# A fused attention and gated feed-forward kernel: output layer of tiles 2 to 8 in seven block products, mask as a matmul, new scheduler priorities

## Chip, cores and metric

The kernel runs on one core of one Trainium2 chip. The metric is the device time of one execution in microseconds. A profiled execution gives a span, from the first to the last instruction that the profile shows, and a time of its own that includes what lies around the span.

## What is computed

Causal attention with a sliding window of 64 over 8 batches of 8 heads, 576 positions and head size 64; then its output, as 4608 tokens by 512, goes through a gated feed-forward layer of width 1536. Inputs and output are float32. From the reference:

```python
scores = scale * np.matmul(q, k.transpose(0, 1, 3, 2))
rel = pos[:, None] - pos[None, :]
mask = (rel >= 0) & (rel < window)
scores = np.where(mask, scores, -1000000000.0)
...
attn = attn / (np.sum(attn, axis=-1, keepdims=True) + 1e-09)
...
x = np.ascontiguousarray(attn_out.transpose(0, 2, 1, 3)).reshape(B * S, H * D)
gate = np.maximum(x @ w_gate, 0.0)
val = x @ w_val
return (gate * val @ w_out).astype(np.float32)
```

## The kernel before

The 4608 tokens are nine tiles (0 to 8) of 512 tokens. For each tile there are three stages. *Attention* works on windows of 64 queries that see 128 keys: score matmuls for 8 windows of one half of the heads (`score_run`, L301) go to four PSUM banks, one for each of four heads, because a head's 64 channels lie as 32 rows times two and each row group of 32 rows is a head; ScalarE takes the exponential (L547), VectorE multiplies by the band of ones (L550), TensorE multiplies with the values (`value_block`, L310), VectorE divides by the row sums (L320) and transposes into the tile's activations `xt` (L325). *The hidden layer* (`fast_hidden`, L704) splits tokens, channels and hidden units in halves and makes both products, gate and value, by Winograd's form of Strassen's method: seven block products for eight, with differences of x (L619) and of the weights (L691) as operands. Its sums pass from PSUM through float32 buffers `pr`: ScalarE copies (L750), VectorE adds (L757), ScalarE applies the ReLU (L766, L788) and GpSimd multiplies gate and value into `g_sb` (L775). *The output layer* (`output`, L799) is a plain product: per 128 tokens 12 matmuls of 512 columns into one bank (L815), one copy by ScalarE (L824), one store issued by SyncE (L828). Tile 0 has its own way through the hidden layer (`direct_block`, L638), in which it waits for the weights to load, and the first 384 of its tokens are attended in `first_part` (L327), written out by hand; there the mask is added already in front of the scores, as a matmul of `ident` with `bias` (0 inside the band, -30000 outside).

All else is laid out by a planner (`Plan`, L39) while the program is built. Every operation has a key, a due time in microseconds; an engine that comes free in the planner's own clock takes the ready operation with the lowest key, if the PSUM banks and buffers that it takes are free. So keys are priorities: they set the order of the instructions on each engine, which on the chip is fixed. Keys are derived from `T1` and `STEP` (L127): tile t's hidden layer is due from `T1 + STEP (t - 1)`, its output is spread over the following step (L844). The planner also counts a port that VectorE and GpSimd share (L178). Eight PSUM banks are shared by everything, one of them first of all for the output; 12 buffers `p` hold weights of the attention, 12 float32 buffers `pr` the hidden layer's partial results, 3 float32 buffers `o_sb` the outputs.

GpSimd also issues the loads; SyncE issues the stores and the moves of values inside SBUF (L523).

## Time and profile before

| | us |
|---|---|
| median of 3 runs (313.9 to 316.3) | 314.2 |
| the profiled execution | 314.14 |
| its span | 312.4 |
| TensorE matmuls busy | 297.9 |
| GpSimd busy | 235.6 |
| VectorE busy | 231.8 |
| ScalarE busy | 212.1 |

Costliest groups, busy microseconds: GpSimd's products of gate and value (L775) 121.4 in 96; output matmuls (L815) 107.1 in 456; VectorE's sums (L757) 94.1 in 144; ScalarE's copies (L750) 80.0 in 144; the hidden layer's matmuls (L742) 201 in 1344, in four groups. The page calls TensorE's matmuls PE and its weight loads PEld, VectorE DVE, ScalarE ACT, GpSimd POOL, SyncE SP. A group's mean is how long one instruction lasts; matmuls overlap, so what one adds to a stream is less than its mean and is read from the length of a row of them.

### The profile page before, as it was taken

How to read it: one execution, taken by the hardware profiler on the slowest of the kernel's cores; microseconds unless marked ns; L12 is line 12 of the kernel's file. 1: busy time of each engine (PE TensorE's matmuls, PEld its weight loads, DVE VectorE, ACT ScalarE, POOL GpSimd, SP SyncE). 2: the span in 40 equal slices, each digit the busy share in tenths (PEclk: the TensorE clock that was granted, in tenths of full speed). 3: DMA queues.
4: the chain of work that ended last, by engine and by line, in shares of the span. 5: the costliest groups of instructions: out<-in, count | busy, mean ns of one | idle time of the engine just before them, and what ended most of it. 6: DMA issues, size and time to landing. Idle time of an engine off the chain costs nothing.

```text
span 312.4 us, 10351 instructions
## 1 busy us (share of the span) xinstructions
PE 297.9 (95%) x4341; PEld 213.6 (68%) x4341; DVE 231.8 (74%) x420; ACT 212.1 (68%) x414; POOL 235.6 (75%) x239
## 2 busy tenths in 40 slices
PE   4889989889999999999999999999999999999995
PEld 2566845767767776777777776776687777677754
DVE  6979999989979984799489948894687578524420
ACT  3544282878678669866887688658966986676641
POOL 8798995969997997699679966994569546945440
PEclk9999999999999999999999999999999999999999
DMA  7999999798259925984496549563010110000013
GB/s 218 187 196 208 186 207 209 165 140 69 50 97 196 114 67 106 171 114 66 86 186 94 75 75 162 83 80 70 36 38 36 37 36 36 36 34 36 34 67 103
DMA packets 56126, 32.81 MB, mean 105 GB/s; under 512 B 39440, under 2 KB 47504, under 8 KB 56080
## 3 DMA queue, kind: packets, MB, share of 16 engines
q0 software_dynamic: 46672, 18.29, 49.7%
q1 hardware_dynamic: 9408, 13.87, 13.7%
q8 instruction: 34, 0.56, 0.7%
q14 instruction: 12, 0.10, 0.1%
HBM read 37.75 MB, written 9.44 MB: 151 GB/s over the span
## 4 chain that ended last, share of the span: by engine, by line
PE 76%; DVE 11%; POOL 4%; DMA 3%; issue 3%; ACT 2%; ACTq 0%; POOLq 0%; DVEq 0%
PE bank L742 42%; PE bank L815 25%; PE bank L651 3%; DVE p L550 3%; PE bank L313 3%; DMA wv<-in_moe_w_val_dram 3%; PE bank L307 3%; DVE g_sb L662 2%; POOL v L286 2%; DVE qT L283 1%; POOL g_sb L775 1%; DVE kT L283 1%; DVE pr L757 1%; DVE xw L320 1%; DVE us L691 1%
## 5 line engine op out<-in xcount | busy, mean ns | idle before, releaser
L775 POOL TENSOR_TENSOR g_sb<-pr,pr 128x512 f16<-128x512 f32 x96 | 121.4, 1282 | 56.3 <-ACT pr L766 40.0
L757 DVE TENSOR_TENSOR pr<-bank,pr 128x512 f32<-128x512 f32 x144 | 94.1, 678 | 36.7 <-PE bank L742 31.3
L815 PE MATMUL bank<-wo,g_sb 128*128 128x512 f16 (+2 forms) x456 | 107.1, 368 | 0.2 <-POOL g_sb L775 0.2
L750 ACT COPY pr<-bank 128x512 f32<-128x512 f32 x144 | 80.0, 594 | 31.2 <-PE bank L742 24.6
L815 PEld LDWEIGHTS <-g_sb 128*128 128x128 f16 x456 | 43.3, 98 | 32.9 <-POOL g_sb L775 0.7
L742 PE MATMUL bank<-xt,us 128*128 128x256 f16 x384 | 57.2, 273 | 1.1 <-DVE pr L757 0.8
L742 PE MATMUL bank<-xt,vs 128*128 128x256 f16 x384 | 57.2, 273 | 0.0
L766 ACT ACTIVATE pr<-pr 128x512 f32<-128x512 f32 x72 | 45.9, 637 | 7.3 <-DVE pr L757 6.5
L550 DVE TENSOR_TENSOR p<-p,mask 128x512 f16<-128x512 f16 (+1 forms) x68 | 33.5, 518 | 22.7 <-ACT p L547 22.4
L742 PEld LDWEIGHTS <-us 128*128 128x128 f16 x384 | 36.7, 98 | 11.9 <-issue 1.0
L742 PE MATMUL bank<-xt,wg 128*128 128x256 f16 x288 | 43.3, 273 | 0.0
L742 PE MATMUL bank<-xt,wv 128*128 128x256 f16 x288 | 43.2, 273 | 0.0
L742 PEld LDWEIGHTS <-vs 128*128 128x128 f16 x384 | 37.0, 98 | 8.4
L824 ACT COPY o_sb<-bank 128x512 f32<-128x512 f32 (+2 forms) x38 | 21.6, 567 | 25.7 <-PE bank L815 24.7
L547 ACT ACTIVATE p<-bank 128x512 f16<-128x512 f32 (+1 forms) x68 | 36.0, 594 | 4.3 <-PE bank L307 4.0
L286 POOL DMA_DIRECT2D v<-in_v_dram x40 | 35.0, 878 | 0.2 <-issue 0.2
L788 ACT ACTIVATE pr<-bank 128x512 f32<-128x512 f32 x48 | 27.9, 600 | 9.2 <-PE bank L742 7.4
L742 PEld LDWEIGHTS <-wv 128*128 128x128 f16 x288 | 27.9, 98 | 5.3
L742 PEld LDWEIGHTS <-wg 128*128 128x128 f16 x288 | 27.1, 98 | 5.6 <-ACT pr L750 0.2
L320 DVE TENSOR_TENSOR xw<-bank,r 128x448 f16<-128x448 f32 (+2 forms) x45 | 25.7, 572 | 1.1
L325 DVE STREAM_TRANSPOSE xt<-xw 128x512 f16<-128x512 f16 (+2 forms) x38 | 25.6, 677 | 1.0 <-ACT xw L416 0.3
L619 POOL TENSOR_TENSOR xt<-xt 128x512 f16<-128x512 f16 x16 | 18.5, 1156 | 3.5 <-DVE r L566 3.5
(69 smaller groups left out, 253.4 us busy)
## 6 DMA issues: line engine op xcount, KB each, us to landing
out_dram<-o_sb SPq DMA_DIRECT2D x35, 256.0 KB, 2.3
k<-in_k_dram POOLq DMA_DIRECT2D x15, 288.0 KB, 6.2
q<-in_q_dram POOLq DMA_DIRECT2D x15, 288.0 KB, 6.9
v<-in_v_dram POOLq DMA_DIRECT2D x32, 128.0 KB, 4.9
v<-v SPq DMA_DIRECT2D x12, 132.0 KB, 2.5
v<-v SPq DMA_DIRECT2D x24, 66.0 KB, 2.0
wg<-in_moe_w_gate_dram POOLq DMA_DIRECT2D x6, 256.0 KB, 6.4
wv<-in_moe_w_val_dram POOLq DMA_DIRECT2D x6, 256.0 KB, 8.5
```

Source lines behind the costliest of these rows:

```text
L286: nc.gpsimd.dma_start(v16s[b % 2][lo:hi, g, :, 0:64], v[b, :, 64 * g - 64 + lo:64 * g - 64 + hi].rearrange("h p d -> p h d"))
L320: nc.vector.tensor_tensor(x, blocks_of(to, n)[:, :, 0:D].rearrange("p s (c e) -> p s e c", e=2), r[:, :, :, None].to_broadcast([128, n, 2, ...
L325: nc.vector.transpose(xt[:, 2 * hh:2 * hh + 2, c0:c0 + n].rearrange("p e (s c) -> p s e c", c=32), x)
L547: nc.scalar.activation(pp[g][:, 0:n].rearrange("p n c -> p (n c)"), st[g][:, 0:64 * n], ACT.Exp, scale=scale)
L550: VEC[e].tensor_tensor(pp[g][:, 0:n], pp[g][:, 0:n], mask[:, None, :].to_broadcast([128, n, 64]), MUL)
L742: nc.tensor.matmul(slot[to][:, HT * m:HT * m + HT], w[:, kk, 128 * m:128 * m + 128], x[:, kk], start=(first and m == 0 and kk == 0), stop= ...
L750: lambda e, hold=hold, slot=slot: nc.scalar.copy(hold["x"], slot["A"]),
L757: nc.vector.tensor_tensor(hold["x"], slot[to], hold["x"], ADD)
L766: lambda e: nc.scalar.activation(hold["x"], hold["x"], ACT.Relu), after=[o])
L775: lambda e: VEC[e].tensor_tensor(gh[:, fs:fs + 2, h], pair(a["x"]), pair(b["x"]), MUL),
L788: lambda e, hold=hold, slot=slot, i=i: nc.scalar.activation(hold["x"], slot["A"], ACT.Copy if i else ACT.Relu),
L815: nc.tensor.matmul(bank["b"][:, 0:c1 - c0], gs[t % 2][:, f, 128 * sub:128 * sub + 128], wo[:, f, c0:c1], start=(j == 0 and i == 0), stop=( ...
```

## The change

The output of tiles 2 to 8 is made by the same seven-product form (`fast_output`). With G the gated activations, split in halves of tokens and of hidden units (a11, a12 for the first 256 tokens, a21, a22 for the others), and W the output weights, split in halves of hidden units and of output channels (b11 to b22), it forms s1 = a21 + a22, s2 = s1 - a11, s3 = a11 - a21 (in the place of a21), s4 = a12 - s2 on VectorE, and once for all tiles four such sums of W (`w_sums`; one of them takes the place of b12). Each of the seven products is two groups of six matmuls of 256 columns. P1 = a11 b11, P6 = s2 t2, P7 = s3 t3 and P4 = a22 t4 gather in one bank (A), P2 = a12 b21 in a second, P5 = s1 t1 and P3 = s4 b22 in a third. ScalarE copies bank A after P1 and P6 and the third after P5, VectorE adds the other part from PSUM, and each quarter of the tile's output (256 by 256) is stored by itself; the last quarter of tile 8 in two pieces. The copies are held in the `pr` buffers, which tiles 0 and 1 now use for their outputs too; `o_sb` is gone, and `p` has 10 buffers for 12.

The mask of all other scores is now added as in `first_part`: eight matmuls per run put the transposed bias in front of the scores, so the multiplication on VectorE goes. The transposed bias is made once at the start. Values of one tile are chained in order. Nearly all keys are read from a table `K`; lines that differ in this alone are left out below, as are the names that follow from the rest.

```diff
@@ -16,6 +16,9 @@
+K = {"T1": 51.41, "STEP": 29.49, "wo1": 25.6, "wo2": 25.6, "q0": 3.01, "q1": 6.54, "q10": 3.96, "q11": 8.54, "v": 8.09, "v1": 9.34, "ql": 13.25, "qt": 9.67, "qti": 4.47, "vl": 12.65, "vc": 8.45, "vm": -3.3, "e": 2.08, "gap": 0.57, "gap1": -0.86, "r": -0.33, "tn": -0.21, "xf": 14.83, "wf": 1.51, "wfj": 2.98, "sn": 0.92, "su": 0.25, "re": 17.48, "mu": -1.5, "la": -9.73, "o0": 21.5, "o0j": 2.66, "o0s": -0.82, "oo": 0.049, "os": 0.292, "oj": 1.05, "gs": 0.96, "fo": 0.07, "fi": 0.074, "fs": 0.87, "fu": -1.36, "W0": 86.73, "TF": 2, "rs": 3.83, "rv": 12.34, "rt": -0.03, "d2": 10.31}
@@ -229,15 +232,16 @@
     kTs = [sb(f"kT{i}", [2, 64 + S, 2]) for i in range(2)]
     v16s = [sb(f"v16_{i}", [NG, H, VW]) for i in range(2)]
     nat = {(name, hh): sb(f"{name}{hh}", [S // 32 * D]) for name in "kq" for hh in range(2)}
-    ps = [sb(f"p{i}", [8, 64]) for i in range(12)]
+    ps = [sb(f"p{i}", [8, 64]) for i in range(10)]
     xw = sb("xw", [32, 2, D // 2])
     rw = [sb(f"r{i}", [32, 1], FP32) for i in range(2)]
     xs = [sb(f"xt{i}", [4, TT]) for i in range(4)]
     gs = [sb(f"g_sb{i}", [NF, TT]) for i in range(2)]
     prs = [sb(f"pr{i}", [TT], FP32) for i in range(12)]
-    os_ = [sb(f"o_sb{i}", [DM], FP32) for i in range(3)]
+    ss, ts = sb("ss", [3, HF, HT]), sb("ts", [3, HF, DM // 2])
     mask = consts.tile([128, 64], FP16)
     bias = consts.tile([128, 64], FP16)
+    biasT = consts.tile([128, 2, 128], FP16)
     ident = consts.tile([128, 128], FP16)
     zero = consts.tile([128, 512], FP16)
     zero32 = consts.tile([128, 384], FP32)
@@ -299,13 +303,21 @@
         return kTs[b % 2][rows, hh, 64 * w:64 * w + 128], qTs[b % 2][rows, hh, 64 * w:64 * w + 64]
 
     def score_run(st, items, biased=False):
+        n = len(items)
+        if not biased:
+            for s in range(2):
+                for g in range(G):
+                    rows = slice(32 * g, 32 * g + 32)
+                    nc.tensor.matmul(st[g][:, 0:64 * n].rearrange("p (n c) -> p n c", c=64)[:, :, 32 * s:32 * s + 32],
+                                     biasT[rows, s], ident[rows, None, rows].to_broadcast([32, n, 32]),
+                                     start=(s == 0), stop=False, skip_group_check=True)
         for i, (win, hh) in enumerate(items):
             for dh in range(2):
                 for g in range(G):
                     kk, qq = scores_of(win, hh, g)
                     c = 64 * i
                     nc.tensor.matmul(st[g][:, c:c + 64], kk[:, :, dh], qq[:, :, dh],
-                                     start=(dh == 0 and not biased), stop=(dh == 1), skip_group_check=biased)
+                                     start=False, stop=(dh == 1), skip_group_check=True)
 
     def value_block(to, c, p, win, hh, at, s):
         b, w = divmod(win, NG)
@@ -354,6 +366,12 @@
 
         st = banks[0:4], banks[4:8]
         rounded("k", nc.vector.tensor_copy, nc.scalar.copy)
+        for s in range(2):
+            for g in range(G):
+                nc.tensor.matmul(banks[6 + s][32 * g:32 * g + 32, 0:128], bias[:, 32 * s:32 * s + 32], ident,
+                                 start=True, stop=True, skip_group_check=True)
+        for s in range(2):
+            nc.scalar.copy(biasT[:, s], banks[6 + s][:, 0:128])
         for u in range(2):
             for g in range(G):
                 nc.tensor.matmul(st[u][g][:, 0:2 * U].rearrange("p (n c) -> p n c", c=64), ident,
...
@@ -450,8 +468,8 @@
             return pe(k * w * (n + 6) / 2400.0)
 
         T0 = 16.0
-        T1 = 49.0
-        STEP = 31.0
+        T1 = K["T1"]
+        STEP = K["STEP"]
 
         def period(t):
             return T1 + STEP * (t - 1)
...
@@ -537,20 +555,16 @@
             batches = sorted({w // NG for w, _ in items})
             halves = sorted({hh for _, hh in items})
             after = [turns[b, nm, hh] for b in batches if b for hh in halves for nm in "kq"]
-            run = op("scores", key, pe(0.0081 * 8 * n), lambda e: score_run([st[g] for g in range(G)], items),
+            run = op("scores", key, pe(0.0081 * 8 * n + 0.0268 * n), lambda e: score_run([st[g] for g in range(G)], items),
                      after=after, take=[("bank", st, range(G))])
             for b in batches:
                 score_ops[b].append(run)
-            masks = []
+            exps = []
             for g in range(G):
                 def exp(e, g=g):
                     nc.scalar.activation(pp[g][:, 0:n].rearrange("p n c -> p (n c)"), st[g][:, 0:64 * n], ACT.Exp, scale=scale)
-
-                def band(e, g=g):
-                    VEC[e].tensor_tensor(pp[g][:, 0:n], pp[g][:, 0:n], mask[:, None, :].to_broadcast([128, n, 64]), MUL)
-                x = op("exp", key + 0.8 + 0.6 * g, act(64 * n), exp, after=[run], take=[("p", pp, (g,))], give=[("bank", st, g)])
-                masks.append(op("mask", key + 2.0 + 0.8 * g, dve16(64 * n), band, after=[x]))
-            return pp, masks
+                exps.append(op("exp", key + K["e"] + 0.6 * g, act(64 * n), exp, after=[run], take=[("p", pp, (g,))], give=[("bank", st, g)]))
+            return pp, exps
 
         def value_bank(t, key, parts, before, gives, last):
 
...
@@ -822,14 +840,109 @@
 
                     def evac(e, bank=bank, o_sb=o_sb, c0=c0, c1=c1):
                         nc.scalar.copy(o_sb["o"][:, c0:c1], bank["b"][:, 0:c1 - c0])
-                    x = op("evac", key, act(c1 - c0), evac, after=before, take=[("o", o_sb, ("o",))], give=[("bank", bank, "b")])
+                    x = op("evac", key, act(c1 - c0), evac, after=before, take=[("pr", o_sb, ("o",))], give=[("bank", bank, "b")])
                     rows = slice(TT * t + 128 * sub, TT * t + 128 * sub + 128)
                     op("store", key + 0.5, {"SP": (0.35, False)},
                        lambda e, o_sb=o_sb, rows=rows, c0=c0, c1=c1: nc.sync.dma_start(out[rows, c0:c1], o_sb["o"][:, c0:c1]),
-                       after=[x], give=[("o", o_sb, "o")], dma=(0.26 * (c1 - c0) / DM, 0.3, "sp"))
-
-        last_part = []
-        output(0, lambda sub, j: T0 + 19.0 + 3.6 * j + 0.9 * sub, range(4))
+                       after=[x], give=[("pr", o_sb, "o")], dma=(0.26 * (c1 - c0) / DM, 0.3, "sp"))
+
+
+        low, high = slice(0, HF), slice(HF, NF)
+        HD = DM // 2
+        wsums = []
+
+        def w_sums():
+
+            b11, b12, b21, b22 = (wo[:, f, HD * d:HD * d + HD] for f in (low, high) for d in range(2))
+            before = [o for blk in range(NF // 4) for o in loaded["o", blk]]
+            direct_out = [o for t in range(TF) for o in out_ops[t]]
+            for c in range(NJ):
+                fs = slice(2 * c, 2 * c + 2)
+                made = []
+                for n, (to, x, y) in enumerate(((ts[:, 0], b12, b11), (ts[:, 1], b22, ts[:, 0]), (b12, b22, b12), (ts[:, 2], b21, ts[:, 1]))):
+                    after = before + [[], made[0:1], made[0:1] + direct_out, made[1:2]][n]
+                    made.append(op("wo_form", W0 + 4 * c + n, {**pool(512), **dve16(512)},
+                                   lambda e, to=to, x=x, y=y, fs=fs: VEC[e].tensor_tensor(to[:, fs], x[:, fs], y[:, fs], SUB), after=after))
+                wsums.extend(made)
+
+        def fast_output(t, key_of):
+
+            mine = out_ops.setdefault(t, [])
+            gt = gs[t % 2]
+            a11, a21, a12, a22 = (gt[:, f, HT * h:HT * h + HT] for f in (low, high) for h in range(2))
+            g11, g21, g12, g22 = ([gates[t, j, n, h] for j in range(NJ)] for n in range(2) for h in range(2))
+            done = out_ops.get(t - 1, [])
+            key = key_of(0)
+            sums = [[], [], [], []]
+            for c0, c1 in ([(2 * j, 2 * j + 2) for j in range(NJ)] if t == LAST else [(0, HF)]):
+                c = slice(c0, c1)
+                made = []
+                for n, (to, x, y, how) in enumerate(((ss[:, 0], a21, a22, ADD), (ss[:, 1], ss[:, 0], a11, SUB), (a21, a11, a21, SUB), (ss[:, 2], a12, ss[:, 1], SUB))):
+                    js = slice(c0 // 2, c1 // 2)
+                    after = [g21[js] + g22[js], g11[js] + made[0:1], g11[js] + made[0:1], g12[js] + made[1:2]][n] + done
+                    made.append(op("g_sum", key - K["gs"] + n, {"DVE": (0.11 + 0.0006 * (c1 - c0) * HT, True)},
+                                   lambda e, to=to, x=x, y=y, how=how, c=c: VEC[e].tensor_tensor(to[:, c], x[:, c], y[:, c], how), after=after))
+                    sums[n].append(made[n])
+            b11, b12, b21, b22 = (wo[:, f, HD * d:HD * d + HD] for f in (low, high) for d in range(2))
+            s1, s2, s3, s4 = sums
+            what = {"P1": (a11, b11, g11), "P2": (a12, b21, g12), "P3": (ss[:, 2], b22, s4), "P4": (a22, ts[:, 2], g22 + wsums),
+                    "P5": (ss[:, 0], ts[:, 0], s1 + wsums), "P6": (ss[:, 1], ts[:, 1], s2 + wsums), "P7": (a21, b12, s3 + wsums)}
+            bank, hold, snaps, ran = {}, {}, {}, {}
+            mine += [o for some in sums for o in some]
+
+            def leave(after, x, h, d, m0, m1, key):
+                rows = out[TT * t + HT * h + 128 * m0:TT * t + HT * h + 128 * m1, HD * d:HD * d + HD].rearrange("(m p) c -> p m c", p=128)
+                src = x["x"] if False else None
+                return op("store", key, {"SP": (0.35, False)},
+                          lambda e: nc.sync.dma_start(rows, x["x"][:, HD * m0:HD * m1].rearrange("p (m c) -> p m c", c=HD)),
+                          after=after, give=[("pr", x, "x")] if m1 == 2 else (), dma=(0.13 * (m1 - m0), 0.3, "sp"))
+
+            place = 0
+            for name in ("P1", "P2", "P6", "P5", "P7", "P3", "P4"):
+                a, b, after = what[name]
+                to = {"P2": "B", "P5": "C", "P3": "C"}.get(name, "A")
+                first = name in ("P1", "P2", "P5")
+                after = list(after)
+                if name in ("P6", "P7", "P3"):
+                    after.append(snaps[{"P6": "P1", "P7": "P6", "P3": "P5"}[name]])
+                if name == "P4":
+                    after += ran["C22"]
+                parts = []
+                for m in range(2):
+                    def mm(e, a=a, b=b, to=to, first=first, m=m):
+                        for f in range(HF):
+                            nc.tensor.matmul(bank[to][:, HD * m:HD * m + HD], a[:, f, 128 * m:128 * m + 128], b[:, f],
+                                             start=(first and m == 0 and f == 0), stop=(f == HF - 1), skip_group_check=True)
+                    k = key_of(place)
+                    place += 1
+                    parts.append(op("o" + name, k, direct(HD, 1, HF), mm, after=after + parts,
+                                    take=[("bo+bank" if to == "A" else "bank", bank, (to,))] if first and m == 0 else ()))
+                mine += parts
+                if name in ("P1", "P6", "P5"):
+                    x = hold[name] = {}
+                    snaps[name] = op("snap", k - K["fs"], act(512), lambda e, x=x, to=to: nc.scalar.copy(x["x"], bank[to]),
+                                     after=parts, take=[("pr", x, ("x",))])
+                    continue
+                src, h, d = {"P2": ("P1", 0, 0), "P7": ("P5", 1, 1), "P3": ("P6", 0, 1), "P4": (None, 1, 0)}[name]
+                x = hold.get(src, {})
+                ran[name] = []
+                for m0, m1 in ((0, 1), (1, 2)) if t == LAST and name == "P4" else ((0, 2),):
+                    c = slice(HD * m0, HD * m1)
+                    give = [("bank", bank, to)] if name != "P7" and m1 == 2 else ()
+                    if src:
+                        o = op("osum", k - K["fu"], dve(HD * (m1 - m0)),
+                               lambda e, x=x, to=to, c=c: nc.vector.tensor_tensor(x["x"][:, c], bank[to][:, c], x["x"][:, c], ADD),
+                               after=[snaps[src]] + parts[m0:m1], give=give)
+                    else:
+                        o = op("evac", k + 0.9, act(HD * (m1 - m0)), lambda e, x=x, to=to, c=c: nc.scalar.copy(x["x"][:, c], bank[to][:, c]),
+                               after=parts[m0:m1], take=[("pr", x, ("x",))] if m0 == 0 else (), give=give)
+                    if name == "P7":
+                        ran["C22"] = [o]
+                    leave([o], x, h, d, m0, m1, k + 0.5)
+
+        TF = int(K["TF"])
+        W0 = K["W0"]
+        output(0, lambda sub, j: T0 + K["o0"] + K["o0j"] * j + K["o0s"] * sub, range(4))
         made = 1
         for t in range(1, NT):
             while made < B and made * NG < 8 * t + 8:
@@ -841,10 +954,14 @@
             pieces = ((0, DM),)
             P = period(t + 1)
             if t < LAST:
-                output(t, lambda sub, j: P + STEP * (0.06 + 0.25 * sub) + 0.9 * j, range(4))
+                if t == TF:
+                    w_sums()
+                if t < TF:
+                    output(t, lambda sub, j: P + STEP * (K["oo"] + K["os"] * sub) + K["oj"] * j, range(4))
+                else:
+                    fast_output(t, lambda i: P + STEP * (K["fo"] + K["fi"] * i))
             else:
-                output(t, lambda sub, j: P + 2.7 * sub + 0.9 * j, range(3))
-                output(t, lambda sub, j: P + 2.7 * 3, range(3, 4), ((0, 256), (256, 384), (384, 512)))
+                fast_output(t, lambda i: P + 0.66 * i)
         end = plan.run(lambda o, e: o.fn(e))
         return plan
```

## Prediction

> **What bounds the kernel now.** I read the engines' totals, then busy time by stage, then the chain of work that ended last, then groups of instructions, and last the timeline for single intervals. The totals:
>
> ```profile
> PE 297.9 (95%) x4341; PEld 213.6 (68%) x4341; DVE 231.8 (74%) x420; ACT 212.1 (68%) x414; POOL 235.6 (75%) x239
> ```
>
> TensorE is busy 95% of the span; its weight loads lie beside its matmuls. Busy time by stage (length, then PE, PEld, DVE, ACT, POOL, each with its instructions):
>
> ```profile
> 0.00:18.50 18.50, 11.67 (x262) 6.92 (x263) 13.23 (x32) 8.71 (x28) 15.02 (x29) 1.00 1.28 199
> 18.50:40.00 21.50, 21.50 (x306) 16.31 (x303) 20.73 (x40) 8.99 (x20) 19.83 (x25) 1.00 1.39 199
> 40.00:59.00 19.00, 17.36 (x285) 10.45 (x283) 18.63 (x32) 10.94 (x20) 14.85 (x17) 1.00 1.20 202
> 59.00:90.46 31.46, 28.96 (x519) 21.65 (x518) 27.94 (x50) 24.86 (x49) 27.94 (x28) 1.00 0.65 84
> 90.46:122.18 31.72, 31.45 (x466) 22.42 (x464) 26.20 (x46) 23.15 (x46) 28.46 (x29) 1.00 0.75 119
> 122.18:153.90 31.72, 31.72 (x475) 23.22 (x473) 24.79 (x45) 23.75 (x46) 26.79 (x27) 1.00 0.76 111
> 298.69:312.40 13.71, 10.42 (x72) 5.91 (x70) 0.89 (x2) 3.30 (x7) 2.92 (x3) 1.00 0.26 90
> ```
>
> From 122 us to 298.7 PE never idles: a tile takes 31.72 us because that is its matmul work. PE idles 6.8 us in the first 18.5, then 1.64 + 2.50 + 0.27 = 4.4 us up to 122, and 3.3 us at the end. Between 18.5 and 90 us DVE is almost as full as PE; later it has 7 us free per tile. Is a busy PE at its pace? Pieces of the chain of waits (start, length, count):
>
> ```profile
> 134.49 4.37 PE bank L742 x40
> 298.69 7.79 PE bank L815 x36
> ```
>
> A 256-column matmul takes 4.37/40 = 0.1093 us, a 512-column one 7.79/36 = 0.2164. Time per column is the same, so columns are what costs. The clock column is 1.00 throughout.
>
> **The change, part by part**, against the profiled execution: span 312.40, 314.14 with the 1.74 around it (the median of the runs is 314.2).
>
> *Seven products for eight, tiles 2 to 8.* Per tile 48 matmuls of 512 columns, 48 x 0.2164 = 10.39 us, become 7 products x 2 token blocks x 6 = 84 of 256 columns, 84 x 0.1093 = 9.18. Their shape (128*128, 128x256 f16) is that of L742, so the price is a row of this trace. Tile 8, whose last block was cut in three, went from 10.42 to 9.18. 7 x 1.21 = **-8.5 us**, all on the path.
>
> *Mask in front of the scores.* Each run of scores (two per tile, 16 in all, and a half-size one for tile 0) gets 8 matmuls of 256 columns that contract 32 rows, in four row groups into four banks, like the scores behind them. The trace has no 256-column one of this kind. The nearest row is the score run itself:
>
> ```profile
> 157.32 0.68 PE L307 MATMUL bank<-qT,kT 32*128 32x64 f16 x64
> 157.93 0.61 PE L742 MATMUL bank<-xt,vs 128*128 128x256 f16 x4
> ```
>
> 64 matmuls of 64 columns, and the next begins 0.61 us after the first; less some 0.12 for leaving, 0.49. One at a time they would take 64 x 0.1093/4 = 1.75. Lower bound, four abreast: 2 x 0.109 = 0.22 per run; upper, one at a time: 0.87. I take 0.23, the scores' way: 16 x 0.23 + 0.12 = **+3.8 us** (3.6 to 14).
>
> The mask multiplications leave DVE (L550, 32.1 + 1.4 us). After 122 us that buys PE nothing directly. Values now wait for the exps alone.
>
> *New vector work per tile:* four f16 sums over 1536 elements on DVE and three additions out of PSUM (0.678 each by L757, 2.0 together). ACT has three copies and one eviction at 0.59 where it had four evictions. A clean 512-element f16 operation takes 0.42 us and a 256-element one 0.28 (shortest L550 records), so 1536 take 0.42 + 4 x 0.14 = 0.96, four 3.8. DVE goes from 24.8 to 24.8 - 3.5 (masks in one period) + 3.8 + 2.0 = 27.1 of a period of 31.72 - 1.21 + 0.46 = 31.0: covered by 3.9 us of slack. What eats that cover:
>
> ```profile
> L550 DVE TENSOR_TENSOR p<-p,mask 128x512 f16<-128x512 f16 x64 | 32.1, 528 | 22.2 <-ACT p L547 21.9
> 153.75 0.42 DVE L550 TENSOR_TENSOR p<-p,mask 128x512 f16<-128x512 f16 x1
> 44.69 2.40 DVE L550 TENSOR_TENSOR p<-p,mask 128x512 f16<-128x512 f16 x3
> 45.14 1.33 POOL L691 TENSOR_TENSOR us<-wg 128x512 f16<-128x512 f16 x1
> ```
>
> The first mask ran alone and took 0.42; the three at 44.69, of which two ran into POOL arithmetic, took 0.80 each on average. POOL's arithmetic (12 products at 1.28, four forms at 1.16) fills some 20 of 31 us, so two or three of four sums meet it and wait about half an operation: +1.8, DVE 28.9. I take no cost for PE; bounds 0 to 9 us, below. The Trainium skill, "SBUF — State Buffer", section "Who interferes with whom", states it as a lock: a DVE instruction with two SBUF inputs and a GpSimd one that reads SBUF exclude each other, the later waits for the whole of the earlier. The trace agrees (0.42 against 0.80), and by that rule the DVE load would be the 28.9, at worst the figure of the third case.
>
> *Sums of the output weights:* 12 once; in the built program 5 stand on POOL (5 x 1.2) ahead of and between tile 1's products, 7 on DVE (2.9 us). Against them tile 1's four x differences go from POOL to DVE (-4.6, +1.7). POOL +1.4 net: no cost.
>
> *Buffers.* Outputs share the 12 f32 buffers of the hidden layer (there were 3 more), and a product set holds two PSUM banks for one. Cover: ACT waits only 4.6 us in all for such buffers now. No cost taken; what it costs if the cover goes is in the second case.
>
> *Start.* Eight small matmuls and two ACT copies (0.27 each, the 128x128 row of L824) come before the first scores; ACT is idle 0.69 us there waiting for q. PE later waits 0.48 and 0.62 us for the value weights, which bounds the hidden delay to about 0.6. The POOL queue that issues that load is unchanged. 0 (to +0.5).
>
> *Order.* In the built program PE changes between wide and small matmuls 68 times instead of 78. Entering costs about 0.10 (in the trace the first score starts 205 ns after a wide matmul, the next wide one 109), leaving about 0.01: 5 pairs, **-0.5**. The 4.4 us of early idle: the first hidden sum (L757) stood behind 12 masks on DVE, 7.2 us with their waits (1.4 and, from 40 to 47.5 us, 5.8); now behind four x differences instead. But 1.8 of the PE waits are TensorE's own issue inside L307, which no order removes. **-1.5** (0 to -2.5).
>
> *End.* P6 of the last tile needs two DVE sums behind the last POOL product. The first matmul behind the hidden layer starts at 298.52, the last POOL product ends at 297.88 + 3.73 = 301.6, two sums of 0.42 and hand-overs: 302.5. PE can bridge with P1, P2 and the six matmuls of tile 7 that the program has between them, 30 x 0.109 = 3.3, to 301.8. Stall 0.7; the last two stores together are larger by 128 KB against what was spread before: 0.2. **+0.9** (0 to 2.5).
>
> Sum: 312.4 - 8.5 + 3.8 - 0.5 - 1.5 + 0.9 = 306.6, and 1.74 around: **308.3 us**.
>
> **The rivals.** *First, the sum holds* (0.62): its own range 306 to 311.
>
> *Second, part comes back as waits of PE on DVE, POOL and buffers* (0.2). For: 90 to 186 us, where POOL has 26 to 28.5 us per tile and each blocked product adds up to 0.96. At four per tile POOL reaches 30 to 32 of 31.0; shared buffers pass this on by the wait ACT on POOL (L750 on L775), then PE on ACT. Three tiles x 1 us and a last-tile stall of 2.5 instead of 0.7: 313, spread 310 to 315. Against: PE idle was 0 here with 5 us of POOL slack.
>
> *Third, DVE becomes the bound* (0.06). If every sum waits out a whole product, 4 x (0.96 + 1.28) = 9.0, DVE has 24.8 - 3.5 + 9.0 + 2.0 = 32.3 us per tile; it decides from 31.0, a mean sum of 1.9 us. Six periods x 1.3 and 1 us at the end: 317.
>
> *Fourth, the bias matmuls run one at a time* (0.07): 0.87 for 0.23 per run, 16 x 0.64 = +10.2: 318.7, slower than before. It decides from a run of 0.59 us, where 16 runs more eat the 5.8 us gain. For: long streams of 256 columns in one row group have no row here. Against: same shape and banks as the scores, which overlap.
>
> *Fifth, narrow matmuls lose to their weight loads* (0.01): a load takes 98 ns, a 256-column matmul hides it by 11. Uncovered even by 20 ns each, 588 x 0.02 = +12: 320. Row L742 excludes it. The Trainium skill, "TensorE: Matmul & The Clock Gate", section "Back-to-back issue gap", gives a sustained 81 ns at 128 columns and 131 at 512; interpolated (an estimate of mine from that page) 98 at 256, so 48 x 131 = 6.3 would become 84 x 98 = 8.2 us, 13 more over seven tiles. The trace disagrees with 216 and 109.
>
> The remaining 0.04 is more early idle recovered: 305.
>
> **How the numbers follow.** Forecast 308.3, the likeliest. 305.5 to 314 leaves out about half of the 0.04 below, the upper quarter of the second case and cases three to five above: 0.2. One per cent of 314.14, about what a measurement of this kernel can tell from no change, sets the bounds 311.0 and 317.3. Faster: 0.62 + 0.04 + 0.04 of the second = 0.70. Within: 0.16 + 0.04 of the third = 0.20. Slower: 0.02 of the third + 0.07 + 0.01 = 0.10.
>
> **What would show it.** Output matmuls of tiles 2 to 8: 588, 0.109 apart. A period near 31.0 us with PE idle 0 after 122. Time from the first bias matmul to the first score: 0.23 right, 0.87 the fourth case. The f16 sums at 0.96 to 1.3 (first), 1.9 (third). New lines "PE on ACT" or "PE on DVE" among the waits after 90 us show the second. Last hidden matmul to last matmul: 9.85 plus a stall below 1. The sum is wrong if PE's busy time does not fall by about 5 us, or if it falls and its idle rises.

## Result and profile after

The changed kernel takes **317.41 us** (median of 20 runs, 315.7 to 322.9). The kernel before, beside it on the same chip, takes 315.19 (313.7 to 318.4). The ratio is 1.0065, with a 95% interval from 1.0037 to 1.0093: two thirds of a per cent slower, where 1.9% faster was forecast, and outside the range. Each ratio and its interval leave out the executions that lie over 1.5% above the fastest of their kernel; medians and ranges keep all. The profiled execution took 317.1 us, of which 315.0 are its span.

In the lines below, L311 is the mask's matmuls, L319 scores, L325 values, L760 the hidden layer's matmuls, L775 its sums, L793 the gate products on GpSimd, L865 the sums of the output weights, L884 the four sums of a tile's activations, L914 the seven products, L923 the copies and L934 the additions of their results. The engines' totals, as shown of before:

```profile
PE 295.2 (94%) x4713; PEld 242.3 (77%) x4713; DVE 262.0 (83%) x421; ACT 215.3 (68%) x414; POOL 238.8 (76%) x240
```

TensorE's (PE's) busy time fell by 2.7 us although its work fell by more, because 3.4 us of it ran at half clock. Its idle time rose from 14.5 to 19.8 us. Where, the busy time by stage says. The stages run from one tile's first hidden matmul to the next one's; columns are length, then PE, PEld, DVE, ACT, POOL, then PE's granted clock. After:

```profile
0.00:18.50 18.50, 11.19 (x241) 6.96 (x242) 12.90 (x32) 9.15 (x30) 14.80 (x29) 1.00 1.29 197
18.50:49.30 30.80, 27.81 (x560) 19.78 (x558) 25.63 (x46) 14.19 (x27) 27.81 (x34) 1.00 1.34 198
49.30:82.30 33.00, 31.57 (x486) 23.10 (x482) 31.51 (x51) 23.08 (x44) 27.63 (x28) 1.00 0.84 124
82.30:113.80 31.50, 30.57 (x482) 22.86 (x480) 27.55 (x43) 24.38 (x47) 29.51 (x29) 1.00 0.77 117
113.80:148.60 34.80, 32.57 (x519) 27.16 (x518) 31.69 (x45) 23.17 (x45) 26.47 (x26) 0.95 0.72 101
148.60:180.20 31.60, 31.29 (x526) 27.35 (x525) 29.20 (x44) 24.42 (x46) 27.35 (x26) 1.00 0.77 115
180.20:211.20 31.00, 31.00 (x526) 27.39 (x525) 28.67 (x44) 24.53 (x46) 23.74 (x23) 1.00 0.51 89
...
242.00:272.80 30.80, 30.80 (x527) 27.21 (x525) 24.01 (x39) 24.50 (x46) 20.99 (x18) 1.00 0.11 36
...
300.30:315.00 14.70, 10.11 (x92) 8.66 (x89) 7.77 (x16) 3.42 (x7) 2.02 (x2) 1.00 0.30 98
```

The same cuts of before, the first four:

```profile
0.00:18.50 18.50, 11.67 (x262) 6.92 (x263) 13.23 (x32) 8.71 (x28) 15.02 (x29) 1.00 1.28 199
18.50:53.60 35.10, 33.46 (x540) 22.14 (x537) 34.02 (x64) 16.14 (x31) 29.85 (x36) 1.00 1.40 200
53.60:79.90 26.30, 24.10 (x433) 18.98 (x432) 24.78 (x46) 20.38 (x40) 22.22 (x23) 1.00 0.85 132
79.90:111.30 31.40, 30.83 (x466) 22.40 (x465) 28.11 (x47) 23.93 (x46) 29.23 (x30) 1.00 0.75 115
```

Length less PE gives the idle time. Up to tile 3's first hidden matmul it is 6.8 + 1.6 + 2.2 + 0.6 = 11.2 us before and 7.3 + 3.0 + 1.4 + 0.9 = 12.7 after. Read from their ends, the stages give three stretches:

- At tile 2 (79.9 against 82.3 us) both have done the same, but for four and a half runs of mask matmuls. They cost 1.0 (4.5 x 0.23); after is 2.4 behind.
- The stage of tile 3 (113.8 to 148.6) takes 34.8 us, where 31.72 - 1.21 + 0.46 = 31.0 was costed. Its clock column is 0.95.
- From 180 us the forecast is met: 31.0 and 30.8 us a tile with PE never idle. Too little is left to earn the loss back.

What happened in the stage of tile 3, on VectorE (DVE), GpSimd (POOL) and PE in the timeline (start, length, instruction, count, idle time before it and what ended it):

```profile
121.47 0.95 DVE L884 TENSOR_TENSOR g_sb<-g_sb 128x1536 f16<-128x1536 f16 x1
...
122.34 3.88 DVE L884 TENSOR_TENSOR ss<-g_sb,ss 128x1536 f16<-128x1536 f16 x1
...
122.88 2.52 POOL L793 TENSOR_TENSOR g_sb<-pr,pr 128x512 f16<-128x512 f32 x2
...
124.33 0.40 PE L311 MATMUL bank<-ident,biasT 32*128 32x256 f16 x8
...
124.56 0.68 PE L319 MATMUL bank<-qT,kT 32*128 32x64 f16 x64
...
126.14 1.27 DVE L775 TENSOR_TENSOR pr<-bank,pr 128x512 f32<-128x512 f32 x2
...
126.87 0.60 PE L760 MATMUL bank<-xt,us 128*128 128x256 f16 x4 [1.63 <-DVE pr L775]
...
128.07 0.60 PE L760 MATMUL bank<-xt,wg 128*128 128x256 f16 x4 [0.60 <-DVE pr L934]
```

A sum of activations takes 0.95 us alone. The next one took 3.88: by its record it began 0.5 us before the first of two GpSimd products, and it ends only 0.8 us after both, one behind the other, are through (122.88 + 2.52 = 125.4). The hidden layer's sums stand behind it in VectorE's queue, so a PSUM bank comes free late and TensorE stands still for 1.63 + 0.60 = 2.2 us. Then the granted clock was 0.5 from 128.64 to 132.05 us, 3.41 us, which costs about 1.7 (half of it). Together 3.9, the whole excess of the stage. The same happened on a smaller scale at 62.87 us, where a sum of output weights took 2.64 us for 0.42 and a hidden matmul waited 0.83 (one in the same place had waited 0.85 before).

Whether such a stop is followed by half clock depends on where it falls. In every trace with several stretches at 0.5 their starts lie whole multiples of 3.41 us apart (20.48 us, six of them, in four traces): the clock goes by windows of that length. In the window ahead of 128.64 TensorE was busy 1.18 of 3.41 us. From 20 us on to the last matmuls, every window of the traces with less than 1.5 us of busy TensorE was followed by one at half clock, those with 1.5 to 1.8 sometimes; a stop that lies across two windows can go free, as one of 2.58 us did ("The old due times" below).

The other early stop has no releaser:

```profile
45.16 1.46 PE L833 MATMUL bank<-wo,g_sb 128*128 128x512 f16 x6
46.55 0.27 PE L325 MATMUL bank<-v,p 128*32 128x65 f16 x10
48.61 0.57 PE L325 MATMUL bank<-v,p 128*32 128x65 f16 x47 [1.79 <-issue]
```

A run of value matmuls breaks off after ten of 72, and the view names nothing that is waited for ("issue"). Counting matmuls from the start, such stops stand at 223 + a multiple of 128 in both kernels: 607 and 991 before, 607, 735 and 1631 after (the last is 1630 in the records, of which some can be missing). 128 matmuls with their weight loads are 256 instructions, and the transfers on the instruction queue number 34 before and 37 after (4341 and 4713 x 2 / 256 = 33.9 and 36.8). So TensorE's instructions seem to be fetched in blocks of 256. The DMA records of the traces bear it out. Each of these transfers is 16384 bytes, and numbering them from 0, matmul 223 + 128n never starts sooner than 1.2 us after the end of transfer n, in any of the 18 traces. At the stops behind the first it starts 1.2 to 1.6 us after it: they are waits for instructions (refills). The stop above ends at 48.61, 1.33 us after a transfer that ended at 47.28. Times from start to start:

| kernel, matmul at which the block ends | block took, us | gap after it, us | from the end of the transfer to the next matmul, us |
|---|---|---|---|
| before, 607 / 991 | 4.0 / 2.8 | 0.96 / 1.17 | 1.46 / 1.54 |
| before, 735 / 1119 | 8.2 / 5.3 | 0.00 / 0.00 | 3.59 / 1.94 |
| after, 607 / 735 | 3.9 / 3.9 | 0.67 / 1.99 | 1.41 / 1.33 |
| after, 991 / 1631 | 5.3 / 4.7 | 0.00 / 1.14 | 1.85 / 1.43 |

Apart from the first (223), stops of over 0.3 us came only behind blocks that were used up in less than 5.7 us, but not behind each of these: in the run with the mask alone, one took 3.9 us up to 1631 and no stop followed. The mask's matmuls add instructions and the searched due times put 64-column matmuls side by side; that this is what makes more blocks go fast was not tested by itself.

### The profile page after: what moved, and what is told of

It is laid out like the page before. It is cut to its first block, busy times and chain, and to the rows that moved or that the text cites. A ratio compares the mean times of both kernels' runs of the same rounds, so it can differ in the third digit from the quotient of the medians.

```text
span 315.0 us, 11158 instructions
## 1 busy us (share of the span) xinstructions
PE 295.2 (94%) x4713; PEld 242.3 (77%) x4713; DVE 262.0 (83%) x421; ACT 215.3 (68%) x414; POOL 238.8 (76%) x240
## 4 chain that ended last, share of the span: by engine, by line
PE 82%; DVE 8%; DMA 4%; issue 3%; ACT 1%; POOL 1%; ACTq 0%; DVEq 0%
PE bank L760 44%; PE bank L914 19%; PE bank L669 7%; PE bank L833 4%; PE bank L325 4%; DMA v<-v 2%; PE bank L319 2%; DVE qT L287 1%; DMA vs<-in_k_dram 1%; PE bank L311 1%; DVE ss L884 1%; DVE kT L287 1%; DVE pr L775 1%; DVE xt L337 1%; DVE xt L635 1%
## 5 line engine op out<-in xcount | busy, mean ns | idle before, releaser
L793 POOL TENSOR_TENSOR g_sb<-pr,pr 128x512 f16<-128x512 f32 x96 | 123.2, 1300 | 38.4 <-ACT pr L784 17.9
L775 DVE TENSOR_TENSOR pr<-bank,pr 128x512 f32<-128x512 f32 x144 | 93.3, 681 | 28.0 <-PE bank L760 27.6
L760 PE MATMUL bank<-xt,us 128*128 128x256 f16 x384 | 56.8, 273 | 1.9 <-DVE pr L775 1.9
L784 ACT ACTIVATE pr<-pr 128x512 f32<-128x512 f32 x72 | 45.2, 638 | 18.5 <-DVE pr L775 18.3
L760 PE MATMUL bank<-xt,vs 128*128 128x256 f16 x384 | 57.0, 274 | 0.0
L760 PE MATMUL bank<-xt,wg 128*128 128x256 f16 x288 | 42.9, 273 | 1.4 <-DVE pr L775 0.8
L760 PE MATMUL bank<-xt,wv 128*128 128x256 f16 x288 | 43.2, 274 | 0.0
L760 PEld LDWEIGHTS <-us 128*128 128x128 f16 x384 | 37.1, 98 | 7.6 <-issue 2.1
L760 PEld LDWEIGHTS <-vs 128*128 128x128 f16 x384 | 37.1, 98 | 5.3 <-issue 0.2
L565 ACT ACTIVATE p<-bank 128x512 f16<-128x512 f32 (+1 forms) x68 | 37.5, 594 | 3.3 <-PE bank L319 3.3
L914 PEld LDWEIGHTS <-g_sb 128*128 128x128 f16 x336 | 32.8, 99 | 5.0 <-issue 0.8
L914 PE MATMUL bank<-wo,g_sb 128*128 128x256 f16 x252 | 33.7, 276 | 0.7 <-ACT pr L923 0.7
L760 PEld LDWEIGHTS <-wg 128*128 128x128 f16 x288 | 27.7, 98 | 5.3 <-issue 1.6
L760 PEld LDWEIGHTS <-wv 128*128 128x128 f16 x288 | 28.2, 98 | 4.2 <-issue 0.2
L914 PEld LDWEIGHTS <-ss 128*128 128x128 f16 x252 | 24.5, 98 | 3.0 <-DVE ss L884 0.2
L833 PE MATMUL bank<-wo,g_sb 128*128 128x512 f16 x96 | 23.2, 379 | 0.0
L914 PE MATMUL bank<-ts,ss 128*128 128x256 f16 x168 | 22.4, 273 | 0.0
```

The costliest lines, as they stand in the source:

```text
L565: nc.scalar.activation(pp[g][:, 0:n].rearrange("p n c -> p (n c)"), st[g][:, 0:64 * n], ACT.Exp, scale=scale)
L760: nc.tensor.matmul(slot[to][:, HT * m:HT * m + HT], w[:, kk, 128 * m:128 * m + 128], x[:, kk], start=(first and m == 0 and kk == 0), stop= ...
L775: nc.vector.tensor_tensor(hold["x"], slot[to], hold["x"], ADD)
L784: lambda e: nc.scalar.activation(hold["x"], hold["x"], ACT.Relu), after=[o])
L793: lambda e: VEC[e].tensor_tensor(gh[:, fs:fs + 2, h], pair(a["x"]), pair(b["x"]), MUL),
L833: nc.tensor.matmul(bank["b"][:, 0:c1 - c0], gs[t % 2][:, f, 128 * sub:128 * sub + 128], wo[:, f, c0:c1], start=(j == 0 and i == 0), stop=( ...
```

## Experiments

Sixteen kernels. Theory: the change loses time where VectorE's f16 sums stand behind GpSimd's products (the lock), and where refills meet dense small matmuls. Rivals: TensorE waits for the sums themselves; VectorE's load; the mask's matmuls; the searched due times. Single executions vary by several us with the stretches at half clock that they catch, so the medians and intervals carry the verdicts; a profile is used for where, and for how much only inside one stage.

### The sums

Four kernels keep the order of the changed one. The first leaves the activation sums out:

```diff
-   VEC[e].tensor_tensor(to[:, c], x[:, c], y[:, c], how)
+   None
...
-   "P3": (ss[:, 2], b22, s4) ... "P5": (ss[:, 0], ts[:, 0], ...), "P6": (ss[:, 1], ts[:, 1], ...)
+   "P3": (a12, b22, s4) ... "P5": (a21, ts[:, 0], ...), "P6": (a11, ts[:, 1], ...)
```

> The four f16 sums of the gated activations per tile are left out, and P3, P5, P6, P7 read plain quarters of the activations instead; the order of all other instructions is that of the changed kernel. Lock theory (sums wait out POOL's products on DVE, the hidden layer's sums behind them come late, PE stops near 125 us and runs 3.4 us at half clock after it): PE idle from 123 to 160 us falls from 2.5 us to below 0.5, no half clock there, the stop before P7 of the last tile (0.67 us) goes; about 312 us. Rival, issue theory (the loss is TensorE's own issue in runs of small matmuls): the stops stay, 316 to 317.

The second makes them, and no product reads them (only the second pair of lines; s3 is written beside a21, not over it):

> The same sums are made, but nothing reads them: products read plain quarters. Takes away only PE's direct wait for a sum, leaves DVE's load and its meeting with POOL. Lock theory: DVE is late as before, so like the changed kernel within 1.5 us (316 to 317). Rival, direct-wait theory (PE stops because a product needs its sum): like the kernel without sums, about 312.

The third puts a transposition of like length, with one SBUF operand, in their place:

> In place of each sum a VectorE transpose of about the same length (384 float32 elements, some 0.85 us against 0.95) that has one input in SBUF; nothing reads it, products read plain quarters. Transposes never grew beside POOL's work in the traces (0.66 to 0.71 and 1.23 to 1.26 us). Lock theory: like the kernel without sums within 1 us, about 312 to 313. Rival, load theory (DVE is simply too full): like the kernel whose sums are made and unread, 316.

The fourth leaves out the sums of the output weights as well:

> The sums of the output weights are left out as well as those of the gated activations; the products read plain quarters. Same order of everything else. Lock theory: the stop of PE near 65 us (0.8 us in the changed kernel, 2.1 without the activations' sums), which follows a weight sum that VectorE took 2.6 us for, goes; so do the half-clock windows from 60 to 90 us, and the median comes to 310 to 312. Rival, early stops come from TensorE's issue and not from DVE: 315, as without the activations' sums alone.

| kernel | median us (range) | ratio to before [interval] | tile 3's stage, us |
|---|---|---|---|
| changed kernel | 317.41 (315.7 to 322.9) | 1.0065 [1.0037, 1.0093] | 34.8 |
| sums left out | 315.40 (311.5 to 320.3) | 0.9938 [0.9893, 0.9983] | 31.1 |
| made, not read | 321.54 (317.8 to 325.1) | 1.0176 [1.0089, 1.0262] | 34.6 |
| transpositions instead | 316.76 (312.7 to 321.8) | 1.0003 [0.9955, 1.0051] | 30.7 |
| weight sums out too | 314.23 (310.8 to 319.2) | 0.9949 [0.9907, 0.9992] | 31.8 |

The last column is from the profiled executions, and it is the clearest of the table. With the sums unread the stop in that stage stays, 1.69 + 0.60 us, with half clock behind it; TensorE waits 4.8 us in all for hidden sums, in three pieces. So it is not TensorE waiting for a sum's result. Without the sums PE idles 0.2 us from 119 to 150 us, with the transpositions not at all, and neither has half clock there. None of the transpositions grew: 0.54 to 0.58 us each in tiles 2 to 7, beside the same products. That shows the lock as the cause of this stage's loss. The transpositions were shorter than the sums' 0.95 (0.85 was expected), so a part for the load is not excluded.

The times say less. Up to some 119 us no edited instruction runs in the first three kernels, and yet their profiled executions take 37.8 us for tile 1's stage, where the changed kernel's took 33.0: refills, waits and half clock differ from one execution to the next. The sums unread cost more than the 316 to 317 expected, with four executions. The transpositions came within 1 us of no sums where the granted clock is equal (mean spans 311.3 and 310.4 without a half-clock stretch, three and two executions); by the medians of all they lie 1.4 apart.

The last row shows that all sums together are worth about 1.2% by the ratios, 0.8% by the medians (314.23 against 314.44 of the kernel before beside it). Its remaining early stops are "issue", 5.2 us, but for one of 0.8 for moved values. Even without a single sum the change gains 0.5% by the ratio and nothing by the medians, where 1.9% was forecast: the rest of the loss is not the sums'.

### The mask

The mask's matmuls left out (so nothing is masked in tiles 1 to 8):

```diff
-        if not biased:
+        if False:
```

> The eight bias matmuls in front of each run of scores are left out, so scores are not masked; all else in the same order. If they cost their columns alone: 16 x 0.23 + 0.12 = 3.8 us less than the changed kernel, about 313.5. Issue theory (they also feed the stops of TensorE's issue): 5 us or more less, and the issue waits of L319 and L325 fall. If PE has other stops there anyway: 2 us or less.

Measured 319.55 us, 1.0158 [1.0095, 1.0221]. The steady periods fell by 0.37 and 0.44 us, two runs at 0.2 as costed, yet the kernel is slower: a stop of 3.6 us at 64 us and one of 1.9 at 128, both for hidden sums. Less work, and a worse meeting.

The mask back on VectorE and GpSimd, with the seven products:

```diff
+   exps.append(op("mask", key + 2.0 + 0.8 * g, dve16(64 * n), lambda e, g=g: band(e, g), after=[x]))
```

> The mask goes back to VectorE's multiplication (no bias matmuls), with the seven products and the new keys. PE has 3.8 us less, DVE 33 us more, all of it with two inputs in SBUF. Lock theory: DVE is late more often, PE stops before 190 us grow from 7 to over 10 us: 320 or more. If TensorE's columns decide: 313.

336.43 us, 1.0677 [1.0636, 1.0717]; stops for hidden sums up to 271 us, and VectorE busy 290.3 of 333.7 us. Products and masks together are too much for VectorE; its load and its waits for GpSimd are not told apart here.

### The output alone

The plain output for tiles 2 to 8, mask and due times as changed:

```diff
-                else:
-                    fast_output(t, lambda i: P + STEP * (K["fo"] + K["fi"] * i))
```

> The mask stays on TensorE and the new keys stay, but tiles 2 to 8 are put out by the plain product, without the sums. By columns alone 8.5 us more of PE than the changed kernel. Lock theory: it loses the 8.5 but has no stops after 90 us and fewer half-clock windows, so it lies near the kernel before: 313 to 317. If the products bring their full gain: 322 or more against the changed kernel's 317.

318.34 us, 1.0112 [1.0068, 1.0156]. The steady period is 32.07 to 32.37 us, so the products bring 1.3 to 1.4 us a tile (1.21 costed). Against the 31.72 of before, mask and due times cost up to 0.65 a tile here; 0.4 is the mask's columns, where the rest comes from is open.

### Moving the refills

24 small matmuls ahead of everything, 48 instructions:

```diff
+        for _ in range(24):
+            nc.tensor.matmul(banks[0][0:32, 0:32], zero[:, 0:32], zero[:, 0:32], ...)
```

> 24 tiny matmuls (48 instructions of TensorE) are added at the start, where PE waits 4.4 us anyway; all else in the same order. Refill theory (TensorE's instructions come by DMA in blocks, and a block's end that falls into a run of small matmuls stops PE, 1.8 us near 46.6): the stop of 1.8 us moves by 24 matmuls out of the run of value matmuls and shrinks below 0.5. If that stop is a wait for data, it stays at 1.8 at the same matmul.

323.81 us, 1.0277 [1.0244, 1.0311]. The stops moved with the count: the block ending at 223 now took 2.4 us and was followed by 1.9 inside the first values, the one ending at 735 took 2.7 and was followed by 3.5, after 50 of 56 values instead of ten of 72. There the transfer began at 47.31, when TensorE had already run out, ended at 48.28, and the next matmul started at 49.71. So the count of instructions places these stops, and they cost more where the block is denser. The expected gain was a miss: this place is worse than the old one.

### Later, and in thirds

The seven products for tiles 5 to 8 only, then the sums of activations in three instructions of 512, then both:

```diff
-"W0": 86.73, "TF": 2
+"W0": 175.2, "TF": 5
...
-   for c0, c1 in ([(2 * j, 2 * j + 2) for j in range(NJ)] if t == LAST else [(0, HF)]):
+   for c0, c1 in [(2 * j, 2 * j + 2) for j in range(NJ)]:
```

> The seven products only for tiles 5 to 8, the plain output for tiles 2 to 4; masks on TensorE and key order as in the changed kernel; the weight sums move to about 175 us. The whole result is computed. Theory (the sums cost a stop only where VectorE has no slack and GpSimd's products come in pairs, and stretches of small matmuls are met by instruction refills only before 135 us): no stop of TensorE over 0.6 us after 112 us, no VectorE sum longer than about 2 us that stops it; four tiles at 30.8 to 31.0 us for 32.1 to 32.4, so span about 315.6 - 4 x 1.3 + 0.8 of tail = 311.2 us without a half-clock window and 313.3 with one; time 313 to 315, about 3 us under the changed kernel and within 0.5% of the kernel before. The early refill stops (at matmuls 607 and 735) stay. Rival (the stop belongs to the first tile with sums, whichever it is): a VectorE sum of 3 to 4 us and a TensorE stop of 1.5 to 2.5 us appear about 210 us with a half clock behind it, and the time is 316 to 318.

> The changed kernel with each of the four sums of a tile's activations made in three instructions of 512 instead of one of 1536, for every tile (12 for 4). The whole result is computed. Theory (a VectorE sum of two SBUF operands is held out while GpSimd's products follow each other): a shorter sum holds GpSimd off for less but waits as long for its turn, and there are three times as many turns; each sum then takes 0.4 us alone (estimate, 0.96 x 512 / 1536 plus a fixed part) and 1.6 to 3 us when met; if the planner can put other VectorE work between them the stop at 127 us shrinks under 1 us and the time is 314.5 to 316. Rival (each turn costs a wait of up to a product): three times the waits, VectorE later still, the stop at 127 us 2.5 us or more, stops in later tiles, 318 us or more.

> Both: seven products for tiles 5 to 8 only, and their sums in thirds. The whole result is computed. If thirds help, up to 1 us under the run with whole sums from tile 5 (312 to 314); if they cost more waits, 1 us or more over it (316). If neither, the sums of the late tiles are hidden either way, and both have the same time within 1 us and the same period of 30.8 to 31.0 us.

From tile 5: the median of six executions is 320.36 us, above what theory and rival gave, and no ratio is on record. The fastest, the profiled one, took 314.32 us, as the theory had it, with no stop over 0.6 us after 112 us but the one at the end (0.67) and no activation sum over 1.92 us; the five others took 320.1 to 321.8 and were not profiled. (Of the weight sums only three moved, to 209 us; the others stayed at 59 to 93, since the planner fills gaps whatever their due time.) Thirds in every tile: 327.57 us, 1.0338 [1.0263, 1.0412], the rival: three times the turns, and stops up to 257 us. Both: 315.86 us, 1.0004 [0.9973, 1.0035], the same as before, though five of its twelve executions took 320.1 to 322.2. In these two profiled executions, with VectorE freed of masks and loads, late sums are hidden, whole or in thirds.

### The old due times

```diff
-K = {"T1": 51.41, "STEP": 29.49, ...}
+K = {"T1": 49.0, "STEP": 31.0, ...}
```

> Of the three parts of the change only the mask on TensorE: the due times (the searched priorities) and the output are those of the kernel before. The whole result is computed. Theory (refills of TensorE's instructions stop it in the early small matmuls, and where they fall is set by the order; the bias matmuls cost their columns): the early stops are those of the kernel before (matmuls 607 and 991, about 1 us each), the period is 31.7 + 0.4 to 0.65 us, span 312.6 + 5 to 6 = 317 to 318.5 without a half-clock window; time 319 to 320. Rival (taking the masks off VectorE and GpSimd gives back the early idle time, as the prediction had it): the idle of tiles 0 to 3 falls under 9 us from 11.2, and the time is 316 to 317.5.

> The changed kernel with the due times of the kernel before wherever there was one (those of the new sums and products stay). The whole result is computed. Theory (what is lost lies in VectorE's sums behind GpSimd's products and in refills, both at places that the order sets): early refill stops at 607 and 991 or 1631, 2 to 3 us in all; whether a sum of the weights or of tile 2 or 3 stops TensorE can't be said from the keys, so span 312 to 316 without half-clock windows, time 315 to 320, within 1% of the changed kernel. Rival (the search for priorities is worth several us and hides a much worse loss): 322 us or more, with stops beyond 150 us. Rival two (the new priorities are themselves the loss): 311 us or less.

> As the run with the old due times, but the seven products for tiles 5 to 8 only. The whole result is computed. Theory: the early part as in the run that moves the mask alone, then three periods of 30.4 to 30.9 and a tail 0.8 longer: its span 2.5 to 4 us under that run, 313.5 to 315.5, time 315 to 317. Rival (sums stop TensorE in whichever tile comes first with them): no gain over the run that moves the mask alone.

The mask alone (buffers and the order of values stay those of the changed kernel): 319.98 us, 1.0130 [1.0079, 1.0181]. The early idle time fell to 9.5 us from 11.2, by 1.7: the term that the prediction had at 1.5. A refill then stopped a run of values at 134 us:

```profile
133.96 0.51 PE L325 MATMUL bank<-v,p 128*32 128x65 f16 x41
137.05 0.42 PE L325 MATMUL bank<-v,p 128*32 128x65 f16 x31 [2.58 <-issue]
```

All of the change under the old due times: 321.18 us, 1.0175 [1.0116, 1.0234], with stops spread to 225 us, between the theory and its first rival. So by the ratios the search is worth 1.1% to the products (1.0175 against 1.0065) and nothing that can be told to the plain output (1.0130 against 1.0112): the due times are not the loss. From tile 5 under the old due times: 325.06 us, 1.0296 [1.0246, 1.0346], far over what any theory gave; its stops are refills (4.9 us) and single waits for VectorE, one of 1.25 at 213 us behind two weight sums that took 3.03.

### The kernel before, changed late

To keep early accidents out, two kernels are the kernel before, instruction for instruction on TensorE up to some 180 and 150 us; then come mask on TensorE (tiles 7 and 8; 6 to 8) and seven products (tiles 5 to 8; 4 to 8).

```diff
+   on_pe = items[0][0] // 8 >= TM
...
-   after = before + [[], made[0:1], ...
+   after = before + [list(out_ops[TF - 2]), made[0:1], ...
```

> The kernel before, instruction for instruction up to about 180 us (same due times, masks by products on VectorE and GpSimd, no bias matmuls), and after that the change: the mask on TensorE for tiles 7 and 8, the seven products for tiles 5 to 8, the sums of the weights in the period of tile 5. The whole result is computed. Theory (the change loses only in the early stage, by where refills and VectorE's sums fall; in late tiles a period takes 30.4 to 30.9 us for 31.7 and the tail 0.8 more): span 312.4 - 1.3 - 0.9 - 1.2 + 0.8 = 309.8 us, time 311 to 312, ratio to the kernel before about 0.992; no stop of TensorE over 0.6 us after 100 us. Rival (a first tile of sums behind GpSimd's products stops TensorE wherever it lies): a sum of 2.5 us or more and a stop of 1.5 to 2.5 us in the period of tile 5 or 6, and the time is 313.5 to 315, no gain.

> The same from one tile earlier: as the kernel before up to about 150 us, then the mask on TensorE for tiles 6 to 8 and the seven products for tiles 4 to 8. The whole result is computed. Theory: one more period at 30.9 for 31.7, 0.9 us under the run from tile 5: span 308.9, time 310 to 311.5, ratio about 0.989. Rival: a stop of 1.5 to 2.5 us where the sums begin (145 to 185 us), time 313 or more.

315.87 us, 1.0045 [1.0022, 1.0069], and 316.81 us, 1.0071 [1.0050, 1.0091]. The rival was right that there is no gain; the stops are smaller than it had them (up to 1.1 us each in both). Stages of the first one, from 143 us, cut as above:

```profile
143.00:174.80 31.80, 31.80 (x475) 23.28 (x474) 24.88 (x45) 23.82 (x47) 26.13 (x26) 1.00 0.70 109
174.80:208.30 33.50, 32.65 (x482) 23.16 (x480) 32.99 (x52) 23.57 (x47) 27.99 (x27) 1.00 0.54 86
208.30:240.70 32.40, 30.91 (x520) 26.52 (x519) 29.01 (x44) 24.18 (x47) 22.88 (x20) 1.00 0.21 41
240.70:271.90 31.20, 31.20 (x527) 27.04 (x525) 23.84 (x39) 24.12 (x46) 19.29 (x17) 1.00 0.11 36
271.90:299.40 27.50, 27.50 (x255) 24.65 (x253) 18.80 (x26) 20.24 (x38) 17.95 (x15) 1.00 0.13 45
299.40:314.10 14.70, 10.12 (x92) 8.68 (x89) 7.78 (x16) 3.42 (x7) 2.01 (x2) 0.99 0.29 98
```

The kernel before, from 174.8 us:

```profile
174.80:206.50 31.70, 31.70 (x475) 23.19 (x473) 24.76 (x45) 23.73 (x46) 25.46 (x25) 1.00 0.64 99
206.50:238.10 31.60, 31.60 (x474) 23.14 (x472) 22.86 (x43) 23.72 (x46) 20.43 (x18) 1.00 0.18 48
238.10:269.80 31.70, 31.70 (x474) 23.16 (x472) 21.53 (x41) 24.52 (x47) 21.01 (x18) 1.00 0.08 29
269.80:298.50 28.70, 28.70 (x218) 21.14 (x217) 11.88 (x19) 20.00 (x38) 16.09 (x14) 1.00 0.10 38
298.50:312.40 13.90, 10.61 (x74) 6.02 (x72) 1.07 (x2) 3.36 (x8) 3.11 (x3) 1.00 0.27 94
```

Up to 174.8 us it is at the same microsecond as before. The stage that takes the weight sums fills VectorE (32.99 of 33.5; single weight sums there took up to 2.2 us for 0.42) and loses 1.8 us, 0.85 of it idle; the first with activation sums loses 0.8. The next two gain 0.5 and 1.2, the end gives back 0.8: +1.7, as the spans differ. The first activation sum of this kernel (its L901, the product L810, the matmul L931):

```profile
214.92 3.73 POOL L810 TENSOR_TENSOR g_sb<-pr,pr 128x512 f16<-128x512 f32 x3
...
216.22 3.25 DVE L901 TENSOR_TENSOR ss<-g_sb 128x1536 f16<-128x1536 f16 x1 [0.27 <-POOL g_sb L810]
...
219.50 0.96 DVE L901 TENSOR_TENSOR ss<-ss,g_sb 128x1536 f16<-128x1536 f16 x1
...
220.52 0.83 PE L931 MATMUL bank<-ts,ss 128*128 128x256 f16 x6 [1.11 <-DVE ss L901]
```

Again one sum waits out two products in a row (to 214.92 + 3.73 = 218.65) and ends 0.8 us behind them, and TensorE stops for 1.1 us, here for the sum itself, with no refill near. The lock is enough without the early stage. No kernel of these that computes the whole result is faster than the one before.

## Why the prediction was wrong

Right, point by point:

- *Columns.* Output matmuls start 109 ns apart (the rival of narrow matmuls is out), and periods of 31.0 and 30.8 us meet the 31.0 costed.
- *Mask in front.* 124.33 to 124.56: 0.23 us from the first mask matmul to the first score, the value taken; the fourth case is out.
- *End, in part.* There is one stall of 0.67 us, where 0.7 was costed. But it is TensorE waiting for a copy (L923) between two products that share a bank, not for sums, so the size was luck. From the last matmul to the end of the span it takes 3.9 us for 3.3, where the stores were to add 0.2.
- *VectorE's load.* 29.2 and 28.7 us in the tiles that run freely, for 28.9. The total was lucky in its parts: not two or three sums waited half an operation each, but one sum per tile waited 1.5 to 1.7 us (2.69 and 2.48 for 0.95).

Three steps failed:

- *New vector work, "I take no cost for PE".* The load was right, the cover was the wrong measure. The wait was taken as half an operation per sum, spread over the period; single sums took 3.88, 2.69 and 2.48 us for 0.95, and the first stood ahead of a hidden sum that freed a PSUM bank. A slack of some 3 us per tile does not cover a wait of 2.9 in one place. Price: 2.2 us of stop in the stage of tile 3. This is the second case, by another way than it named: not through backlog on GpSimd and shared buffers, but through VectorE's queue. The Trainium skill, "SBUF — State Buffer", section "Who interferes with whom", has the later instruction wait for the whole of the earlier. The trace goes beyond it: by the records both products began after the sum, and it ended behind both.
- *Order, "-1.5".* 1.5 us was to come back up to tile 3; 1.4 was added. The mask alone gave 1.7 back, so the reason was sound; refills spent it and more. By what ended it, "issue" had 1.75 of the 11.2 us of idle time before and 4.3 of the 12.7 after; all else together did shrink, by 1.1. The weight sums, "no cost", are not where it went: the matmul that waited 0.83 us behind one (2.64 us for 0.42 at 62.87) stands where one waited 0.85 before, and with the weight sums left out the profiled execution idled no less up to tile 3 (14.6 us). The prediction had seen 1.8 us of "issue" inside the scores and taken it as fixed. It is instructions that come late, and where that falls depends on the order.
- *No term for the clock.* A stop of some 2 us among small matmuls was followed by 3.41 us at half clock, 1.7 us lost. The profile before has none of these up to its last instruction, so nothing was priced. Over the 20 executions of the changed kernel, spans rose with the number of such stretches (read from the mean granted clock): 314.0 us with none, 315.4 with one, 317.6 with two.

Then the sum: 2.9 us missed up to tile 2, 3.8 in the stage of tile 3, 0.6 in that of tile 4, and some 1 us in the order term of -0.5, the end and the rest, of 315.0 - 306.6 = 8.4 us. (A slip that changes nothing: the fourth case's 308.3 + 10.2 is 318.5, not 318.7.)

What stays open: what sets the moment at which a transfer of instructions begins; how much of VectorE's lateness is load beside the lock; and why executions of one kernel (from tile 5) lie 6 us apart, which was not seen in a profile.

## To carry over

Price a new VectorE instruction by the longest single wait that it can meet and by what stands behind it in its queue, not by its mean against the slack of a period. A change that gains 0.8 us a tile on the bound engine over seven tiles does not survive one accident in the first of them; look at the first tile that uses it, where one-time work and loads still fill the other engines. Where a stop shows no releaser, count instructions and look for the transfer that brings them before calling it fixed.

## What the runs showed of the hardware

- TensorE's "issue" stops stand at a fixed count of its instructions, every 256: each block comes in one transfer of 16384 bytes, and its first matmul never started sooner than 1.2 us after the transfer's end. Where 128 matmuls were used up in less than some 5.7 us, the wait for the next block cost up to 3.5 us, though not each time.
- An f16 sum on VectorE with two SBUF operands can be held out by several GpSimd products in a row (3.88 us for 0.95, ending 0.8 us behind the second); a transposition with one operand never was (at most 0.72 us for 512 elements).
- The granted clock falls to 0.5 for 3.41 us at a time or for twice that, in windows that stand whole multiples of 3.41 us apart. The Trainium skill, "TensorE: Matmul & The Clock Gate", section "Part 1: The HAM clock gate (the "warmup" mystery)", has a window of that length. Here stops of some 2 us were enough, where they left TensorE busy less than 1.5 us of one window.
